# Retention, softplus and relu-squared kernel: the head works on 128 tokens as one chunk, and step 0's products come in two halves of the tokens

## The chip, the cores and the metric

The kernel runs on one core of a Trainium2 chip. The metric is device time in microseconds (us) of one execution. Engines are named TensorE (PE in the profile; PEld is its loading of weights), VectorE (DVE), ScalarE (ACT) and SyncE (SP, which here only issues DMAs). A tile in SBUF or PSUM has 128 partitions; "lower" and "upper" are partitions 0 to 63 and 64 to 127.

## The reference

Three stages, all in float32. q, k and v are (4, 8, 576, 64): batch, heads, tokens, head size. x has 2304 rows of 512 columns.

```python
# 1: retention with decay, no softmax
scores = q @ k.transpose(0, 1, 3, 2) / sqrt(64)
gamma = 1 - 2.0 ** (-5 - arange(8))                 # one per head
rel = pos[:, None] - pos[None, :]
ret = (scores * where(rel >= 0, gamma ** rel, 0)) @ v
x = ret.transpose(0, 2, 1, 3).reshape(2304, 512)
# 2: softplus layer, weights 512 x 2048 and 2048 x 512
h = x @ w1_in
x = (maximum(h, 0) + log1p(exp(-abs(h)))) @ w1_out
# 3: relu-squared layer, weights of the same shapes
r = maximum(x @ w2_in, 0)
out = (r * r) @ w2_out
```

## The kernel before, in words

Retention is computed by chunks: within a chunk by masked scores, across chunks by a running state (k times v, 64 x 64 per head). The decay is a weight on v per token and head (table `vw`) and a factor on the result (table in `cst`, one block of 256 columns for each of the nine 64-token blocks of a sequence). The layers work on tiles of 512 or 384 tokens (`TILES`). The second layer's products with float32 accuracy are three products each of rounded parts: high by high, high by low, low by high.

The weights come through SP's queue into a ring of three staging buffers (`load_w`, `pump_load`). `words` makes two passes of ScalarE and one of VectorE over a block, `split_w` then makes its high part on ScalarE and its low part on VectorE; `pump_step` does one of these stages, `pump_begin` begins blocks, `pump_end` ends them and issues the next loads.

The order on every engine is the program's (`manual_schedule`). The head (lines 982 to 1103) makes x for the first 512 tokens, in four chunks of 128. A chunk is loaded by two DMAs of 512 KB on SP's queue (line 362): q and k transposed, lower partitions the first 64 tokens, upper the second, all eight heads side by side; then k and v with tokens on partitions. The opening loads constants on ScalarE's queue, runs 18 warm products of 128 columns (`keep_warm`), spreads two rows of constants over the partitions by products with ones (`spread`, line 963), and makes the factor table from them on VectorE (`make_xw`, line 972: blocks 1, then 2 and 3, then 4 to 8). For each chunk TensorE then computes scores of 64 by 64 tokens (line 1016), the state of the first 64 tokens (line 416), and, interleaved, outputs of both halves (line 439; each half has its own products and, after the first, products with the carried state), the second half's state and the next chunk's scores. VectorE weights v (372), masks the scores (1023), scales the outputs into x (1048) and makes the low part of x (1062); ScalarE copies the state twice a chunk in two pieces (427), casts the high part of x (1052) and issues the store of x (1056). The first block of w1_in is split among the last chunk's work, blocks 1 and 2 behind it.

Then the steps begin: step j computes 12 products of 512 columns (`g1`, line 519), softplus (lines 532 to 545), part of the attention of the next tiles (`attend`), the split of the result (554, 555), and the second product of step j - 2 (`g2`, line 570). In step 0 `g1` needs all 512 tokens' high and low x and the split block 0.

## Time and profile before

| | us |
|---|---|
| three runs | 841.63, 843.45, 843.67 |
| median | 843.45 |
| profiled execution | 842.52 |
| its span, first to last instruction | 840.7 |

The profile is of one execution. "Busy" is the time in which an engine had an instruction in it; for TensorE the ends are modelled, and instructions overlap, so a row's duration of 0.22 us for a small product is its latency and the distance between starts is its cost. Each float32 product stands as two matmul instructions. PEclk is the granted clock of TensorE, 1.00 being full speed; before the first change of the clock that was recorded it reads 1.00. "Issue" in the chain of waits is time in which the engine waited for nothing that the profile shows.

### The profile page before, as it was taken

How to read it: one execution, taken by the hardware profiler on the slowest of the kernel's cores; microseconds unless marked ns; L12 is line 12 of the kernel's file. 1: busy time of each engine (PE TensorE's matmuls, PEld its weight loads, DVE VectorE, ACT ScalarE, POOL GpSimd, SP SyncE). 2: the span in 40 equal slices, each digit the busy share in tenths (PEclk: the TensorE clock that was granted, in tenths of full speed). 3: DMA queues.
4: the chain of work that ended last, by engine and by line, in shares of the span. 5: the costliest groups of instructions: out<-in, count | busy, mean ns of one | idle time of the engine just before them, and what ended most of it. 6: DMA issues, size and time to landing. Idle time of an engine off the chain costs nothing.

```text
span 840.7 us, 16953 instructions
## 1 busy us (share of the span) xinstructions
PE 820.1 (98%) x6189; PEld 731.0 (87%) x6189; DVE 700.3 (83%) x1331; ACT 473.7 (56%) x890; POOL 0.2 (0%) x4
## 2 busy tenths in 40 slices
PE   8889999999999999999999999999999999999998
PEld 7767799988788877888899999988999988999887
DVE  3688888878978888787999988899698997787876
ACT  2699899666666766666888621355321554111553
POOL 0000000000000000000000000000000000000000
PEclk9899999999999999999999999999999999999999
DMA  9556545546556674476686788898988889888885
GB/s 329 178 177 221 187 145 173 179 139 195 187 185 212 199 224 161 149 234 212 206 265 208 238 242 250 248 310 275 305 255 250 250 265 279 290 250 249 252 272 167
DMA packets 121207, 189.44 MB, mean 225 GB/s; under 512 B 10402, under 2 KB 66338, under 8 KB 121122
## 3 DMA queue, kind: packets, MB, share of 16 engines
q1 hardware_dynamic: 118848, 187.21, 70.1%
q10 hardware_dynamic: 2276, 1.14, 0.5%
q8 instruction: 50, 0.82, 0.4%
q14 instruction: 33, 0.27, 0.1%
HBM read 147.41 MB, written 40.89 MB: 224 GB/s over the span
## 4 chain that ended last, share of the span: by engine, by line
PE 82%; DVE 7%; ACT 6%; issue 2%; DMA 1%; ACTq 0%; DVEq 0%
PE acc L570 19%; PE ph L519 18%; PE py L699 9%; PE py L772 9%; PE px L699 6%; PE pz L772 6%; PE px L772 6%; PE pz L699 6%; PE po L439 2%; DVE l L542 1%; ACT l L534 1%; DVE xl L482 1%; DVE e L539 1%; PE st L416 1%; ACT e L533 1%
## 5 line engine op out<-in xcount | busy, mean ns | idle before, releaser
L519 PE MATMUL ph<-xh,wi 128*128 128x512 f32 (+1 forms) x640 | 146.7, 371 | 2.1 <-ACT l L534 1.1
L519 PEld LDWEIGHTS ph<-xh,wi 128*128 128x128 f32 x640 | 117.4, 189 | 18.8 <-issue 1.6
L570 PE MATMUL acc<-gh,woh 128*128 128x512 f32 (+1 forms) x320 | 120.1, 378 | 0.4 <-ACT woh L185 0.4
L570 PE MATMUL acc<-gl,woh 128*128 128x512 f32 (+1 forms) x320 | 118.6, 371 | 1.4 <-DVE gl L555 1.4
L570 PE MATMUL acc<-gh,wol 128*128 128x512 f32 (+1 forms) x320 | 118.1, 369 | 0.7 <-DVE wol L186 0.7
L539 DVE SCALAR_TENSOR_TENSOR e<-e 128x512 f32<-128x512 f32 (+1 forms) x80 | 51.0, 638 | 45.7 <-ACT l L534 44.9
L699 PE MATMUL py<-t,sring 128*128 128x384 f32 x432 | 88.6, 339 | 0.0
L519 PE MATMUL ph<-xl,wi 128*128 128x512 f32 (+1 forms) x320 | 78.9, 367 | 0.1
L532 ACT ACTIVATE e<-ph 128x512 f32<-128x512 f32 (+1 forms) x80 | 44.2, 552 | 58.6 <-PE ph L519 58.2
L699 PEld LDWEIGHTS py<-t,sring 128*128 128x128 f32 x432 | 74.8, 188 | 2.5 <-DVE uring L903 0.5
L752 ACT CAST gh<-g 128x384 fp32r<-128x384 f32 x84 | 43.2, 515 | 46.2 <-PE px L772 16.1
L570 PEld LDWEIGHTS acc<-gl,woh 128*128 128x128 f32 x320 | 60.1, 188 | 10.4 <-DVE gl L555 3.5
L570 PEld LDWEIGHTS acc<-gh,woh 128*128 128x128 f32 x320 | 60.0, 188 | 9.5 <-ACT woh L185 0.8
L570 PEld LDWEIGHTS acc<-gh,wol 128*128 128x128 f32 x320 | 60.1, 188 | 8.9 <-DVE wol L186 1.3
L519 PEld LDWEIGHTS ph<-xl,wi 128*128 128x128 f32 x320 | 58.7, 188 | 8.0 <-DVE xl L482 0.4
L752 ACT CAST gring<-g 128x384 fp32r<-128x384 f32 x84 | 43.2, 516 | 39.9 <-PE py L772 16.2
L899 ACT COPY uring<-px 128x384 f32<-128x384 f32 x24 | 11.5, 479 | 87.3 <-PE px L699 87.3
L699 PE MATMUL pz<-t,sring 128*128 128x384 f32 x288 | 58.3, 334 | 0.0
L699 PE MATMUL px<-t,sring 128*128 128x384 f32 x288 | 58.0, 335 | 0.0
L534 ACT ACTIVATE l<-e,cst 128x512 f32<-128x512 f32 (+1 forms) x80 | 54.5, 681 | 5.8 <-DMA part_d<-xo 1.9
L720 DVE TENSOR_TENSOR gring<-g,gring 128x384 fp32r<-128x384 f32 x84 | 46.2, 553 | 9.8 <-ACT gring L752 8.6
L720 DVE TENSOR_TENSOR g<-g 128x384 f32<-128x384 f32 x96 | 52.6, 554 | 1.5
(116 smaller groups left out, 1635.9 us busy)
## 6 DMA issues: line engine op xcount, KB each, us to landing
sring<-s2d SPq DMA_DIRECT2D x168, 256.0 KB, 3.2
sring<-o2d SPq DMA_DIRECT2D x168, 256.0 KB, 3.5
wi_raw<-in_moe_w_in_dram SPq DMA_DIRECT2D x32, 512.0 KB, 4.6
wo_raw<-in_moe_w_out_dram SPq DMA_DIRECT2D x32, 512.0 KB, 3.7
s2d<-ct SPq DMA_DIRECT2D x48, 256.0 KB, 2.7
o2d<-ct SPq DMA_DIRECT2D x48, 256.0 KB, 2.5
ring<-in_qk_t_dram SPq DMA_DIRECT2D x14, 512.0 KB, 5.2
ring<-in_kv_dram SPq DMA_DIRECT2D x14, 512.0 KB, 6.1
```

The source lines that it names most:

```text
L416: nc.tensor.matmul(st[to, h, :], lhsT=kk[:, hh, :], rhs=sv[:, hh, :], start=m == h == 0, stop=True, skip_group_check=True,)
L439: nc.tensor.matmul(po[(LO, HI)[hh % 2], hh // 2, :], lhsT=before[rows, hh, :] if carried else sv[:, hh, :], rhs=qp[:, hh, :] if carried el ...
L519: nc.tensor.matmul(ph[:, :n], lhsT=a, rhs=x, start=(j == 0), stop=(j == len(todo) - 1))
L532: nc.scalar.activation(out=e, in_=ph[:, :n], func=AF.Abs)
L534: nc.scalar.activation(out=l, in_=e, func=AF.Ln, bias=below_one, scale=1.0 + 2.0**-23)
L539: nc.vector.scalar_tensor_tensor(out=e, in0=e, scalar=-2.0, in1=e, op0=ALU.add, op1=ALU.mult)
L570: nc.tensor.matmul(acc[j][:, :n], lhsT=a, rhs=x, start=(begin and m == 0), stop=(end and m == 2))
L699: nc.tensor.matmul(ps, lhsT=a, rhs=x, start=(first and m == 0), stop=(m == len(todo) - 1), skip_group_check=True,)
L720: nc.vector.tensor_tensor(out=out, in0=a, in1=b, op=ALU.subtract)
L752: nc.scalar.copy(h, src)
L772: nc.tensor.matmul(blocks[m][:, :cols], lhsT=a[:, c], rhs=x, start=(first and p == n == 0), stop=(p == NP - 1 and n == len(todo) - 1), ski ...
L899: nc.scalar.copy(s1, px)
```

## The change

The head keeps its four chunks, but a chunk is one block of 128 tokens. q and k come as two loads of 256 KB each, heads 0 to 3 to the lower and 4 to 7 to the upper partitions, on the queues of SP and ScalarE (chunk 3 on SP alone). Scores are 128 x 128 tokens per head, masked by one 128 x 128 mask (`causal`); the state is made once a chunk from all 128 tokens and copied once (`kept_s`). Scores of even chunks go to two banks of their own, those of odd chunks to the two banks of `ps_h`. Chunk c + 1's scores stand ahead of chunk c's state. The warm products are 6 and 1 of 512 columns in place of 18, 3, 4 and 8 of 128. Blocks 4 to 8 of the factor table are made by ScalarE, four pieces of 128 x 64 each. x is stored from SP's queue. Step 0's `g1` is `early_g1`: tokens 0 to 255 within the head, 256 to 511 at its old place. `g1` of other steps is as before.

```diff
-    first = tc.tile_pool(name="first", bufs=n_first)
+    first = tc.tile_pool(name="first", bufs=2)
...
+    def early_qk(c, g, eng):
+        eng.dma_start(
+            out=qks[c][(LO, HI)[g]].rearrange("p i s h c -> p i s (h c)"),
+            in_=qk_t[2 * c:2 * c + 2].rearrange("s p i h c -> p i s (h c)")[
+                ..., g * HH * CN:(g + 1) * HH * CN
+            ],
+        )
...
+    def early_scores(c):
...
+        for hh in range(HH):
+            for s, to in enumerate((LO, HI)):
+                for g, rows in enumerate((LO, HI)):
+                    nc.tensor.matmul(
+                        pb[g][to, hh * P:(hh + 1) * P],
+                        lhsT=qks[c][rows, 1, s, hh, :], rhs=qks[c][rows, 0, :, hh, :],
...
+    def early_mask(c):
+        mixed[c] = first_pool.tile([P, H, P], F32, tag="mixed", name="mixed")
+        for g, pb in enumerate(pbs[c]):
+            n = H // len(pbs[c])
...
+            nc.vector.tensor_tensor(
+                out=mixed[c][:, g * n:(g + 1) * n], in0=pb,
+                in1=causal.unsqueeze(1).to_broadcast([P, n, P]), op=ALU.mult,
+            )
+
+    def early_states(c):
...
+        for h in range(HH):
+            for to, hh in ((LO, h), (HI, h + HH)):
+                nc.tensor.matmul(
+                    st[to, h, :], lhsT=kvs[c][:, 0, hh, :], rhs=kvs[c][:, 1, hh, :],
...
+        if c + 1 < last:
+            kept_s[c] = first_pool.tile([P, HH, D], F32, tag="kept", name="kept")
+            nc.scalar.copy(kept_s[c], st)
...
+    def early_carried(c):
+        pos[c] = ps_head.tile([P, 2, 512], F32, tag="po", name="po", bufs=1)
+        for h in range(HH if c else 0):
+            for g, rows in enumerate((LO, HI)):
+                nc.tensor.matmul(
+                    early_po(c, g * HH + h),
+                    lhsT=kept_s[c - 1][rows, h, :], rhs=qks[c][rows, 0, :, h, :],
...
+    def early_o(c):
+        for hh in range(H):
+            nc.tensor.matmul(
+                early_po(c, hh), lhsT=kvs[c][:, 1, hh, :], rhs=mixed[c][:, hh, :],
...
+    def early_keep(c):
+        nc.sync.dma_start(out=x0d[:, :, c * P:(c + 1) * P], in_=kept_of[c])
...
+    def early_g1(half):
+        if half == 0:
+            hps[0] = h_bank("ph")
+        c = slice(half * 256, half * 256 + 256)
...
+        todo = sum(todo if half else [todo[0], todo[2], todo[1]], [])
...
+    def scalar_xw(m, n):
+        for m in range(m, m + n):
+            for a in range(KD):
+                nc.scalar.activation(
+                    out=later[:, m - 1, a], in_=cst[:, C_XW + a * CN:C_XW + (a + 1) * CN],
+                    func=AF.Copy, scale=times[:, m - 1, a:a + 1],
+                )
...
+        early_qk(0, 0, nc.sync)
+        early_qk(0, 1, nc.scalar)
+        early_kv(0)
         for half in (LO, HI):
             nc.scalar.dma_start(out=cst[half, :C_XW], in_=consts[CN:P, :C_XW])
...
+        keep_warm(6)
+        early_scores(0)
+        row.append(rows_in.rearrange("p (m a b) -> p m a b", a=KD, b=CN))
+        spread_rows()
+        keep_warm(1)
+        scalar_xw(4, 2)
+        early_mask(0)
+        early_v(0)
         make_xw(1, 1)
+        early_scores(1)
+        early_states(0)
+        early_mask(1)
+        early_v(1)
+        early_carried(0)
+        early_o(0)
+        early_x(0)
+        early_scores(2)
+        early_states(1)
+        scalar_xw(6, 1)
+        early_carried(1)
+        early_o(1)
         make_xw(2, 2)
+        early_mask(2)
+        early_v(2)
+        early_x(1)
+        scalar_xw(7, 2)
+        early_scores(3)
+        early_states(2)
+        early_carried(2)
+        early_o(2)
         early_low(0)
+        early_mask(3)
+        early_v(3)
+        begin_words()
         early_keep(0)
+        early_x(2)
+        next(begun[0])
         early_low(1)
         early_keep(1)
         early_states(3)
+        early_carried(3)
+        early_o(3)
+        next(begun[0])
+        begun.clear()
+        begin_words()
+        early_g1(0)
+        early_x(3)
+        next_state(3, 1)
+        begin_words()
         early_low(2)
+        early_low(3)
         early_keep(2)
+        for made in begun:
+            next(made)
         early_keep(3)
...
-        g1(j, f, n)
+        if j == 0:
+            early_g1(1)
+        else:
+            g1(j, f, n)
```

## Rows read from the trace of the kernel before

**Rows 1.** windows: stretches; per engine busy us and instructions, then clock, DMA

```profile
10.80:31.50 20.70, 17.81 (x521) 16.72 (x520) 12.68 (x19) 9.84 (x24) 0.00 (x0) 0.92 0.62 214
...
50.00:90.00 40.00, 37.84 (x398) 30.37 (x396) 35.90 (x65) 37.27 (x67) 0.00 (x0) 1.00 0.70 235
90.00:840.00 750.00, 740.57 (x5039) 664.50 (x5039) 634.96 (x1217) 410.76 (x775) 0.00 (x0) 1.00 0.71 225
```

**Rows 2.** timeline, opening: start, duration, engine, line, operation, tiles, count

```profile
0.73 0.39 SPq L362 DMA_DIRECT2D ch<-in_qk_t_dram  x1
...
1.04 6.77 PE L946 MATMUL cold<-warm 128*128 128x128 f32 x36 [1.04 <-DVE warm L940]
...
8.60 0.64 PE L963 MATMUL rows<-rows_in,ones 1*64 1x256 f32 x2 [0.15 <-DMA rows_in<-in_consts_dram]
...
10.81 1.15 PE L1016 MATMUL pb<-ch 64*64 64x64 f32 x32
11.88 1.16 PE L946 MATMUL cold<-warm 128*128 128x128 f32 x8
12.97 0.68 PE L416 MATMUL st<-ch 64*64 64x64 f32 x16
```

**Rows 3.** chain of waits in order of time: start, duration, what

```profile
17.07 1.16 issue
...
21.57 1.45 issue
```

**Rows 4.** windows, around the stretch at the lower clock

```profile
19.50:23.30 3.80, 2.35 (x77) 2.09 (x73) 2.68 (x5) 1.98 (x5) 0.00 (x0) 1.00 0.54 183
23.30:26.80 3.50, 3.50 (x106) 3.50 (x99) 0.69 (x1) 1.03 (x3) 0.00 (x0) 0.51 0.02 5
```

**Rows 5.** timeline, last chunk and step 0's products

```profile
29.12 0.69 DVE L1048 TENSOR_TENSOR x<-po,cst 128x512 f32<-128x512 f32 x1 [0.65 <-PE po L439]
...
30.32 0.62 ACT L1052 CAST xh<-x 128x512 fp32r<-128x512 f32 x1
...
31.51 1.20 PE L519 MATMUL ph<-xh,wi 128*128 128x512 f32 x4
...
33.45 1.07 PE L519 MATMUL ph<-xh,wi 128*128 128x512 f32 x4
```

**Rows 6.** timeline, SP's issue of wo0 and ScalarE up to step 1

```profile
30.43 0.33 SPq L137 DMA_DIRECT2D wo_raw<-in_moe_w_out_dram  x1
...
31.36 0.68 ACT L152 ACTIVATE wi_raw<-wi_raw 128x512 f32<-128x512 f32 x1
...
35.27 0.60 ACT L532 ACTIVATE e<-ph 128x512 f32<-128x512 f32 x1
...
41.80 0.62 ACT L185 CAST woh<-ct 128x512 fp32r<-128x512 f32 x1 [3.31 <-DVE ct L157]
```

**Rows 7.** DMA queues and issues of the first 30 us

```profile
q8 instruction: 4, 0.07, 0.9%
...
ch<-in_qk_t_dram SPq DMA_DIRECT2D x4, 512.0 KB, 5.8
...
x0d<-x ACTq DMA_DIRECT2D x3, 256.0 KB, 2.9
```

**Rows 8.** timeline of TensorE where four quarters run

```profile
18.46 0.23 PE L439 MATMUL po<-ch,ring 64*64 64x64 f32 x2
...
18.52 0.23 PE L439 MATMUL po<-ch,ring 64*64 64x64 f32 x2
```

**Rows 9.** groups by form, VectorE: count, busy us, mean ns of one

```profile
L1023 DVE TENSOR_TENSOR ch<-pb,cst 128x512 f32<-128x512 f32 x4 | 2.8, 691 | 3.6 <-PE pb L1016 3.6
...
L972 DVE SCALAR_TENSOR_TENSOR cst<-cst,times 128x1280 f32<-128x1280 f32 x1 | 1.5, 1484 | 0.0
```

**Rows 10.** groups by form, ScalarE up to 35.3 us

```profile
L427 ACT COPY ring<-st 64x256 f32<-64x256 f32 x16 | 5.9, 366 | 11.4 <-PE st L416 11.2
...
L967 ACT COPY times<-rows 128x32 f32<-128x32 f32 x1 | 0.2, 187 | 0.4 <-PE rows L963 0.4
```

More of the change, by code (lines that the diff above doesn't have):

```diff
@@ L512, in g1 @@
                 part.append((a[:, c], x))
-        if key:
-            todo = [[w for two in zip(*todo[:2]) for w in two], todo[2]]
-        else:
-            todo = [todo[0], todo[2], todo[1]]
-        todo = sum(todo, [])
+        todo = [w for two in zip(*todo[:2]) for w in two] + todo[2]
         for j, (a, x) in enumerate(todo):
@@ L956 @@
     times = times.rearrange("p (m a) -> p m a", a=KD)
-    def spread(dst, row, shape, eng):
-        rows = ps_head.tile([P, 512], F32, tag="pb1", name="rows")[:, :shape[0] * shape[1]]
-        rows = rows.rearrange("p (a b) -> p a b", a=shape[0])
-        for half in (LO, HI):
-            one = slice(half.start, half.start + 1)
-            nc.tensor.matmul(
-                rows[half], lhsT=ones[one], rhs=row[one],
-                start=True, stop=True, skip_group_check=True,
-            )
-        eng(dst, rows)
     def make_xw(m, n):
@@ new lines, in early_o, with early_x @@
+    def early_o(c):
+        for hh in range(H):
+            nc.tensor.matmul(
+                early_po(c, hh), lhsT=kvs[c][:, 1, hh, :], rhs=mixed[c][:, hh, :],
+                start=c == 0 and hh % HH < 2, stop=True, skip_group_check=True,
+            )
+    def early_x(c):
+        m = 2 * c
+        if c < last - 1:
+            x = ew.tile([P, 512], F32, tag="e", name="x", bufs=3)
+        else:
+            x = ew.tile([P, 512], F32, tag="l", name="x")
+        kept = x.rearrange("p (a n) -> p a n", a=KD)
+        xs_of[c] = kept
+        table = cst[:, C_XW + m * 256:C_XW + (m + 2) * 256]
+        nc.vector.tensor_tensor(
+            out=x.rearrange("p (g a s b) -> p g a s b", g=2, a=2, s=2),
+            in0=pos.pop(c)[:, :, :256].rearrange("p g (a s b) -> p g a s b", a=2, s=2),
+            in1=table.rearrange("p (s g a b) -> p g a s b", s=2, g=2, a=2), op=ALU.mult,
+        )
+        nc.scalar.copy(early_at(x_hi(), c), kept)
+        kept_of.append(kept)
@@ new lines, in begin_words, with spread_rows @@
+    def begin_words():
+        count, make, args = items[n_split[0]]
+        pump_load(n_used[0] + count)
+        begun.append(make(*args))
+        next(begun[-1])
+        n_split[0] += 1
+        n_used[0] += count
+    row = []
+    def spread_rows():
+        rows = ps_head.tile([P, 2, 512], F32, tag="po", name="rows", bufs=1)
+        to = [
+            rows[:, 0, at:at + n * b].rearrange("p (a b) -> p a b", a=n)
+            for at, n, b in ((0, KD, CN), (256, SCN - 1, KD))
+        ]
+        for half in (LO, HI):
+            one = slice(half.start, half.start + 1)
+            for r, of in zip(to, (row[0][:, 0], row[0][:, 1:, :, 0])):
+                nc.tensor.matmul(
+                    r[half], lhsT=ones[one], rhs=of[one],
+                    start=r is to[0], stop=True, skip_group_check=True,
+                )
+        nc.scalar.copy(cst[:, x_first].rearrange("p (a b) -> p a b", a=KD), to[0])
+        nc.scalar.mul(times, to[1], float(D) ** 0.5)
@@ L984 @@
         for half in (LO, HI):
             nc.scalar.dma_start(out=cst[half, :C_XW], in_=consts[CN:P, :C_XW])
-        for row in (0, CN):
-            nc.scalar.dma_start(
-                out=rows_in[row:row + 1], in_=consts[row:row + 1, C_XW:]
-            )
+        for r in (0, CN):
+            nc.scalar.dma_start(out=rows_in[r:r + 1], in_=consts[r:r + 1, C_XW:])
+        early_qk(1, 0, nc.sync)
+        early_qk(1, 1, nc.scalar)
+        early_kv(1)
+        early_qk(2, 0, nc.sync)
+        early_kv(2)
@@ L999 @@
             )
-        keep_warm(18)
-        row = rows_in.rearrange("p (m a b) -> p m a b", a=KD, b=CN)
-        spread(
-            cst[:, x_first].rearrange("p (a b) -> p a b", a=KD), row[:, 0], (KD, CN), nc.scalar.copy
-        )
-        spread(times, row[:, 1:, :, 0], (SCN - 1, KD), nc.scalar.copy)
-        make_xw(1, 1)
-        keep_warm(3)
-        pbs, pos, xs_of, kept_of = {}, {}, {}, []
-        def early_scores(c, half):
-            if c not in pbs:
-                pbs[c] = in_heads(ps_head.tile([P, 512], F32, tag=f"pb{c % 2}", name="pb"))
-            return [
-                lambda h=h: nc.tensor.matmul(
-                    pbs[c][half, h, :], lhsT=chunk[c][half, 1, h, :], rhs=chunk[c][half, 0, h, :],
-                    start=True, stop=True, skip_group_check=True,
-                ) for h in range(H)
-            ]
@@ L1103 @@
         early_keep(3)
     tc.no_sync_barrier()
-    for c in range(last):
-        chunk.pop(c)
     head.__exit__(None, None, None)
```

152 lines of the change are left out of this document (75 added, 77 removed).

## The prediction

> **What bounds the kernel now.** The page has TensorE busy almost throughout, so I split the span into stretches [rows 1]. From 90 us on TensorE works 740.57 of 750 us; nothing that the change touches lies there, so that part stays as it is. From 50 to 90 TensorE, ScalarE and VectorE are all at 90 to 95%. Only the head (10.8 to 31.5 us, TensorE 17.81 of 20.70, VectorE 12.68, ScalarE 9.84) has room, and as the later work follows it at a fixed distance, a microsecond by which the head ends earlier is a microsecond of the whole, unless step 0 or 1 gets a new wait.
>
> In the head the work is serial; there I went through the timeline and the chain of waits. The first score products start at 10.81, because the warm products and then the row of constants (8.60) hold TensorE [rows 2]. Four chunks follow, each with scores, mask, first state, its copy, second state, its copy, outputs. Twice TensorE stands, for 1.16 and 1.45 us, with nothing that the profile names [rows 3], and for 3.5 us its granted clock is 0.51, the lower of its two levels (1.2 and 2.4 GHz), after a stretch in which it was busy for only 2.35 of 3.80 us [rows 4]. The last chunk's x is made at 29.12, its cast starts at 30.32, and step 0's products run from 31.51 to 34.52 [rows 5]. But ScalarE is what step 0's softplus waits for: it works from 31.36 until it takes up that softplus at 35.27 [rows 6], when the products are already done. So the forecast is the new time of that softplus.
>
> **The change part by part.** All times are for the profiled execution (span 840.7, whole 842.52 us); the median of the three runs shown is 0.9 us above it.
>
> *Opening.* 18 warm products of 128 columns become 6 of 512. Each is two instructions: 36 took 6.77 us [rows 2], 0.19 each; later 8 take 1.09 with a change of form at the end, so about 0.12 without. In pieces of 128 columns the new count is 48, 12 more: 1.4 to 2.3 us, and 0.2 for clearing a wider operand first. I take 1.4, as the last pieces are the fast ones: TensorE is free at 7.8 + 1.6 = 9.4. Scores no longer stand behind the constants, and chunk 0's q and k were to hand by about 6.5 (issue 0.73 [rows 2] plus 5.8 [rows 7]). Scores start at 9.4, not 10.81.
>
> *TensorE in a chunk.* Scores: 16 products of 128 columns, 32 instructions, going round the four quarters of the array. Where all four are in use now, a round of four instructions of 64 columns takes 0.06 us (18.46 to 18.52 [rows 8]); with 128 columns 0.12, so 8 rounds take 1.0. State: 8 products instead of 16, over all 128 tokens; 16 instructions of 64 columns that alternate between two quarters took 0.68 with their tail [rows 2], 0.5 without. Carried: 8 products of 128 columns in four quarters, 0.5. Own: 8 products over all rows, 128 columns, in two halves, 16 x 0.06 = 0.95. Together 2.9 us. If halves did not run side by side, own and state products would take double, 1.4 more a chunk; none would be cheaper than a round. I take the side-by-side figure, which [rows 2] shows for two quarters.
>
> A change of form costs too. From the eight warm products at 11.88 to the state products at 12.97 it is 1.09 us for 8 x 0.11, so 0.2 for going from the full array to quarters; from quarters to the full array it is 0.1 (scores end about 11.77, 10.81 + 1.15 less a tail of 0.19; next start 11.88) [rows 2]. The new chunk changes form four times (quarters, full rows in halves, quarters, full rows), where a chunk kept to quarters before. At 0 to 0.2 each I take 0.17: 0.7 a chunk, 2.7 in all, of which about half falls into waits for VectorE, so 1.3 on the path.
> The Trainium skill, "TensorEngine Tiling (Array Packing)", Tiling Modes, says under its key properties that changing the mode, not just the tile, drains the engine: by it all 16 changes are paid, as in the sum below. The trace shows the drain at the full array (0.1 and 0.2 us), none between quarters and halves; without it the sum would be 1.3 us lower.
>
> *The walk.* 4 x 3.6 us, less the carried part that chunk 0 hasn't (0.7), is 13.7; the constants' products and one more warm product of 512 columns take 2.3 with their changes: 9.4 + 13.7 + 2.3 = 25.4 for the last own product. VectorE beside it: the mask is now 1024 columns wide, 1.22 us by the two widths in [rows 9] (0.69 for 512, 1.48 for 1280); with v, x and the low part at 0.6 (a start every 0.6 us) that is 3.0 a chunk against TensorE's 3.6, so they are hidden, and without that cover each would cost its excess. ScalarE makes 20 pieces of 128 x 64 of the table that VectorE made in one instruction of 1.48 us: 0.19 for 32 columns and 0.37 for 256 [rows 10] put one at 0.2, 4.0 us in all, bounds 2.4 (overlapped) to 5.0. In exchange 16 state copies of 0.37 become 3 single ones and two. The pieces stand in gaps of ScalarE; only the last eight (1.6 us) delay the third state copy, to about 22.6, level with the product that overwrites what it reads.
>
> *Tail.* x of chunk 3 falls behind the low part of wi0 on VectorE and starts at 26.0. Then x 0.69, cast 0.62, low 0.69, with 0.1 between and two others ahead of the last: 28.2. The first half of step 0's products (tokens 0 to 255) needs none of this and runs before; the second half is 12 x 256 columns, 1.4 (8 x 512 took 1.94 in [rows 5]), and 0.2 tail: 29.8, against 34.52. ScalarE from the cast's end (27.3): state copies 0.75, two passes over wi2 1.3, then the casts of wi1 and wi2, the second behind VectorE's 0.69: 30.8. That is the softplus, 4.5 us before 35.27.
>
> *DMAs.* q and k come as eight loads of 256 KB to 64 partitions in runs of 1 KB, not four of 512 KB. Bounds: no slower, or half the rate. At half, 2 MB take up to 5 us more, and the last chunk lands near 18, wi0 near 20; first uses are 19 (scores 3), 21.8 (v 3) and 22.5 (wi0). I take no cost; the cover is one to two microseconds, and a loss beyond it is paid in full. The four stores of x move from ScalarE's queue to SP's, ahead of wo0, wi3 and wo1. wo0 was issued at 30.43 [rows 6], as soon as its buffer was free; now it stands behind the store of chunk 3 (27.4), and the stores (2.9 us each to landing [rows 7]) precede its data: landing near 32.5, when ScalarE is through with the softplus (32.7). A microsecond more would be lost there, but the next cast waits 3.31 us for VectorE anyway [rows 6], so up to that it costs nothing.
>
> *Unnamed waits.* Those of [rows 3] lie one chunk's 128 matmuls apart, and in 30 us four loads of instructions arrive [rows 7]. The new head has some 340 matmuls in place of 570, so I count half a wait: 0.6 us back.
>
> Sum: 4.5 - 0.6 = 3.9 us; 842.5 - 3.9 = 838.6 us (span 836.8).
>
> **The rivals.**
> 1. *More than that:* no changes of form on the path (1.3) and no unnamed wait (0.6): 836.7. For it: quarters run side by side without loss in [rows 8]. Against: TensorE is nearly full in the walk, so any wait adds.
> 2. *Halves don't run side by side:* 1.4 a chunk, 5.6 in all, 1 us of it in waits: gain 3.9 - 4.6, so 843.2, no change. For it: no row shows products of 128 rows in two halves. Against: of 64 rows they do, 16 in 0.5 [rows 2].
> 3. *The clock stays low (slower).* Only 7 of the 33 warm products remain, none after 13 us, and TensorE stops at each mask that is late. A stretch like that of [rows 4] gives away 3.5 x 0.49 = 1.7 us of products, so from the third on the gain is gone. Low from the first scores to the softplus, some 13 us of array work take twice as long; less 1.5 of waits that this covers and the gain it is 13 - 1.5 - 3.9 = 7.6 us slower: 850. For it: such a stretch came in spite of 33 warm products. Against: it followed a wait of 1.45 us and few products; the walk has no gap above 0.5 us.
> The Trainium skill, "TensorE: Matmul & The Clock Gate", HAM oscillation, has idle gaps between bursts of products bring the slow clock back; by it this rival comes if the masks leave such gaps.
> 4. *Moved, not won:* wo0 or the next chunk comes late, and steps 0 and 1 give 2 to 3 us back: 841.2. For it: SP's new order. Against: the 3.31 us of cover.
>
> **How the numbers follow.** Forecast (gain 2.6 to 5.5) 0.58, rival 1 0.14, rival 2 0.10, rival 3 0.07, rival 4 0.11. A measurement can tell 0.3%, 2.5 us, from no change. Faster by more: the forecast, rival 1 and a little of rival 4, 0.74. Within: most of 4 and 2, 0.18. Slower: rival 3 and a bad rival 2, 0.08. The range goes from rival 1 with an opening that wins its bounds and with the overlapped table pieces (another 2.4 us), 834.3, to between rivals 4 and 2, 842.3; rival 3 and the rest of rival 2 are left out.
>
> **What would show it.** The first scores at 9.4; a chunk every 3.6 us (now 4.6); own products 0.06 apart; last x at 26.0; the first softplus at 30.8 with the same 6.5 us from it to the cast now at 41.80. It is wrong if the granted clock shows 0.5 in more than one stretch before 30 us, if scores wait for a load, if TensorE stands over 1 us at the second or third chunk, or if the softplus comes 4 us earlier and the later rows don't.

## The result, and the profile after

The changed kernel takes 848.2 us (median of 9 runs, 845.65 to 851.01), the kernel before 843.45 (9 runs, 841.21 to 845.94): a ratio of 1.0066, 95% interval 1.0045 to 1.0087. It is slower, by 0.7%; the forecast was 838.6 and faster. A ratio is not the quotient of the two medians, so the two need not agree in the last digits.

The profiled execution takes 850.5 us (span 848.7), 8.0 more than that of before. Both kernels take up 80 softpluses in the same order, so the start of each first pass on ScalarE is a clock for the whole program (L532 before, L525 after). After minus before: +0.93 at step 0, then level (+0.90 at step 8), +2.45 at step 9, +4.74 at step 11, +6.36 at step 12, level until step 51, +7.60 at step 52, +8.0 from step 66 on. So one microsecond was lost ahead of step 0, where 4.5 were to be won, and seven in places that the change does not touch.

The windows of [rows 1] show the head still full of waits, with a mean granted clock of 0.84 instead of 0.92 (columns: stretch, its length, busy us and instructions of TensorE, its weight loads, VectorE, ScalarE, GpSimd, then granted clock, DMA share, GB/s):

```profile
10.80:31.50 20.70, 16.70 (x282) 13.08 (x283) 11.74 (x19) 10.53 (x33) 0.00 (x0) 0.84 0.91 264
50.00:90.00 40.00, 37.86 (x404) 30.63 (x400) 35.83 (x65) 37.22 (x67) 0.00 (x0) 1.00 0.71 230
```

The timeline of the opening answers to [rows 2] and shows why. Columns: start, duration, engine (ACTq is ScalarE's queue for DMAs), line, what is done, in brackets the wait before it and what ended it.

```profile
0.72 0.73 ACTq L976 DMA_DIRECT2D qk<-in_qk_t_dram  x1
1.48 1.28 ACTq L1150 DMA_DIRECT2D cst<-in_consts_dram  x2
2.79 0.77 ACTq L1152 DMA_DIRECT2D rows_in<-in_consts_dram  x1
4.65 0.21 ACTq L1152 DMA_DIRECT2D rows_in<-in_consts_dram  x1
7.82 0.63 ACTq L976 DMA_DIRECT2D qk<-in_qk_t_dram  x1
8.54 1.10 PE L998 MATMUL pb<-qk 64*64 64x128 f32 x32
...
12.42 0.43 PE L998 MATMUL pb<-qk 64*64 64x128 f32 x2
...
16.19 1.98 PE L998 MATMUL pb<-qk 64*64 64x128 f32 x30 [3.34 <-DMA qk<-in_qk_t_dram]
18.09 1.12 PE L1030 MATMUL st<-kv 128*64 128x64 f32 x16
19.00 1.92 PE L1054 MATMUL po<-mixed,kv 128*64 128x128 f32 x16
```

The scores of chunk 0 start at 8.54, earlier than forecast. But the upper half of chunk 1's q and k is the sixth load on ScalarE's queue, behind the constants, and the thirteenth of the two queues together. Eight loads are under way at first, four on each queue; by the semaphores in the trace, each later one waits until the load eight places ahead of it, on either queue, has landed. On ScalarE's queue the first four are issued by 3.56, the fifth at 4.65, this one at 7.82, just as the second load of constants, the fifth of all, has landed (7.80). It lands at 16.14, and TensorE stands 3.34 us in the middle of chunk 1's scores. What follows is at the lower of the two clock levels (0.5, 1.2 GHz): 30 score matmuls take 1.98 us and the 16 own products 1.92, against 1.09 for the same 16 in the next chunks. The windows show the level (columns as above):

```profile
14.00:16.00 2.00, 0.00 (x0) 0.00 (x0) 0.00 (x0) 0.00 (x0) 0.00 (x0) 0.81 1.16 205
16.00:18.00 2.00, 1.81 (x30) 1.58 (x30) 0.00 (x0) 0.00 (x0) 0.00 (x0) 0.50 1.11 231
18.00:20.00 2.00, 2.00 (x29) 1.91 (x28) 1.79 (x3) 0.37 (x1) 0.00 (x0) 0.50 1.04 348
20.00:22.00 2.00, 2.00 (x34) 1.67 (x34) 1.12 (x3) 0.31 (x1) 0.00 (x0) 0.50 1.09 347
```

The loads also move fewer bytes per microsecond. From 4 to 16 us the DMA engines are full in both kernels (the last columns: DMA share, GB/s), at 381 GB/s before and 267 in the changed kernel. The kernel before, then the changed one:

```profile
4.00:16.00 12.00, 11.36 (x187) 9.87 (x187) 4.08 (x9) 2.03 (x7) 0.00 (x0) 1.00 1.03 381
```

```profile
4.00:16.00 12.00, 8.49 (x54) 3.91 (x52) 3.08 (x8) 3.77 (x11) 0.00 (x0) 0.97 1.09 267
```

So x of the last chunk comes at 31.59 [rows 5: 29.12] and the softplus at 36.20 [rows 6: 35.27]:

```profile
31.59 0.68 DVE L1068 TENSOR_TENSOR x<-po,cst 128x512 f32<-128x512 f32 x1
32.31 0.62 ACT L1073 CAST xh<-x 128x512 fp32r<-128x512 f32 x1
...
36.20 0.60 ACT L525 ACTIVATE e<-ph 128x512 f32<-128x512 f32 x1
...
42.30 0.62 ACT L185 CAST woh<-ct 128x512 fp32r<-128x512 f32 x1 [2.70 <-DVE ct L157]
```

The later losses are of two kinds. One is the clock again. Between the softpluses of steps 7 and 8 TensorE waits for the splits that ScalarE and VectorE make of the weights and of the softplus, in both kernels in the same way: 1.32 and then 0.64 us busy in two windows of 2 us. In the kernel before the granted clock stays at 1.00 behind this dip:

```profile
88.80:90.80 2.00, 1.32 (x6) 0.69 (x4) 1.93 (x4) 2.00 (x5) 0.00 (x0) 1.00 0.54 191
90.80:92.80 2.00, 0.64 (x2) 0.34 (x3) 2.00 (x4) 2.00 (x4) 0.00 (x0) 1.00 0.00 0
92.80:94.80 2.00, 2.00 (x9) 1.63 (x10) 1.71 (x4) 1.94 (x5) 0.00 (x0) 1.00 0.27 37
```

In the changed kernel the same dip, 0.9 us later, is followed by 0.51, for 3.4 us, and step 9 comes 1.5 us later:

```profile
89.70:91.70 2.00, 1.32 (x6) 0.68 (x4) 1.93 (x4) 2.00 (x5) 0.00 (x0) 1.00 0.60 203
91.70:93.70 2.00, 0.64 (x2) 0.33 (x3) 2.00 (x5) 2.00 (x4) 0.00 (x0) 1.00 0.00 1
93.70:95.70 2.00, 2.00 (x5) 1.54 (x6) 1.72 (x4) 1.94 (x5) 0.00 (x0) 0.51 0.02 8
```

The other kind is a store that lands late. The waits of the changed kernel (engine, its instruction, what it waited for, us in total, times, longest), and then those of the kernel before:

```profile
ACT l L527 <- DMA part_d<-xo: 4.3, 1, 4.3
ACT l L527 <- DMA x2d<-xo: 3.5, 2, 3.3
```

```profile
ACT l L534 <- DMA part_d<-xo: 1.9, 1, 1.9
ACT l L534 <- DMA x2d<-xo: 1.8, 2, 1.6
```

The part sums (step 10) and x2 (step 52) leave by four stores each. ScalarE writes its logarithm into a buffer of the kind from which the second and the fourth go out (`drain_one`), and by the trace it waits until the second has landed: in the kernel before that store is issued at 103.17 and lands 2.03 us later, and the logarithm starts at 105.31. In the changed kernel the DMA view of the five microseconds from the first store has one packet of queue q8 among them, which starts 2.4 us after the first issue, and a median of 4.8 us from issue to landing (columns: queue, packets, MB, share; tiles, queue, count, KB each, us to landing):

```profile
q8 instruction: 1, 0.02, 2.3%
...
part_d<-xo SPq DMA_DIRECT2D x4, 256.0 KB, 4.8
```

In the same stretch of the kernel before no q8 row stands (its load starts 5.4 us after the first store), and the stores take 2.0 us:

```profile
part_d<-xo SPq DMA_DIRECT2D x4, 256.0 KB, 2.0
```

q8 brings instructions: 47 loads of 16 KB for 11,914 matmuls and weight loads of the changed kernel, 50 for 12,378 before, so one for about 250 of them. The change removes 464, and so the loads fall at other points of the program.

Steps 10 to 12 lose 4.0 us in all: 2.4 by this wait, 1.6 because TensorE then stands 2.67 us and the clock falls once more (0.5 for 3.4 us at 114.2). Step 52 loses 1.2 by the second wait.

### The profile page after: what moved, and what is told of

It reads as the page before. It is cut to its first block, busy times and chain, and to the rows that moved or that the text cites. A ratio compares the mean times of both kernels' runs of the same rounds, so it can differ in the third digit from the quotient of the medians.

```text
span 848.7 us, 16501 instructions
## 1 busy us (share of the span) xinstructions
PE 822.5 (97%) x5957; PEld 726.9 (86%) x5957; DVE 702.6 (83%) x1336; ACT 475.1 (56%) x899; POOL 0.2 (0%) x4
## 4 chain that ended last, share of the span: by engine, by line
PE 79%; DVE 8%; ACT 8%; DMA 3%; issue 2%; ACTq 0%; DVEq 0%
PE acc L563 17%; PE ph L512 16%; PE py L692 9%; PE py L765 9%; PE px L692 6%; PE pz L765 6%; PE px L765 6%; PE pz L692 6%; ACT l L527 1%; DVE l L535 1%; DVE e L532 1%; PE po L436 1%; ACT e L526 1%; DVE xl L479 1%; ACT e L525 1%
## 5 line engine op out<-in xcount | busy, mean ns | idle before, releaser
L532 DVE SCALAR_TENSOR_TENSOR e<-e 128x512 f32<-128x512 f32 (+1 forms) x80 | 51.0, 638 | 52.7 <-ACT l L527 51.7
L525 ACT ACTIVATE e<-ph 128x512 f32<-128x512 f32 (+1 forms) x80 | 44.2, 553 | 61.5 <-PE ph L512 60.8
L692 PEld LDWEIGHTS py<-t,sring 128*128 128x128 f32 x432 | 74.9, 188 | 2.6 <-DVE uring L896 0.5
L713 DVE TENSOR_TENSOR gl<-g,gh 128x384 fp32r<-128x384 f32 x84 | 46.6, 556 | 9.1 <-ACT gh L745 8.0
```

The costliest lines, as they stand in the source:

```text
L525: nc.scalar.activation(out=e, in_=ph[:, :n], func=AF.Abs)
L532: nc.vector.scalar_tensor_tensor(out=e, in0=e, scalar=-2.0, in1=e, op0=ALU.add, op1=ALU.mult)
L692: nc.tensor.matmul(ps, lhsT=a, rhs=x, start=(first and m == 0), stop=(m == len(todo) - 1), skip_group_check=True,)
L713: nc.vector.tensor_tensor(out=out, in0=a, in1=b, op=ALU.subtract)
```

## Experiments

Theory A: three things cost the time: the late load, the clock that falls behind waits, and instruction loads that fall into stores. Rivals: the new products or loads are slow as such; or the win is absorbed by full engines later.

Results first; "low" is the sum of the stretches with a granted clock of 0.5 in the first 120 us of the profiled execution (the openings of e13 to e15 are told of below), "softplus" the start of step 0's. Each ratio is to runs of the kernel before that were made along with the version (their medians lie between 841.8 and 843.5).

| kernel | median us | ratio to before, 95% | softplus | low, us |
|---|---|---|---|---|
| before | 843.45 | 1 | 35.27 | 6.8 |
| changed | 848.2 | 1.0066 (1.0045 to 1.0087) | 36.20 | 17.1 |
| e1 load of chunk 1 on SP | 845.09 | 1.0039 (1.0027 to 1.0051) | 32.06 | 10.2 |
| e2 short warm products | 845.07 | 1.0040 (1.0027 to 1.0052) | 35.18 | 13.7 |
| e3 = e1 + e2 | 841.54 | 0.9995 (0.9980 to 1.0011) | 32.03 | 10.2 |
| e5 = e3 + products in step 0's gap | 839.93 | 0.9977 (0.9964 to 0.9990) | 31.22 | 6.8 |
| e6 = e5 + products in step 8 | 840.19 | 0.9972 (0.9958 to 0.9985) | 32.28 | 0 |
| e7 = e3, step 0 not in halves | 841.94 | 1.0003 (0.9984 to 1.0021) | 32.84 | 10.2 |
| e8 = e3 + chunk 2's load on SP | 840.88 | 0.9989 (0.9968 to 1.0011) | 31.53 | 10.2 |
| e10 = e6 + e8 | 839.73 | 0.9964 (0.9948 to 0.9981) | 32.53 | 3.4 |
| e11 = e5 + e8 | 840.88 | 0.9972 (0.9956 to 0.9988) | 31.53 | 3.4 |
| e12 = e10, opening as changed | 841.28 | 0.9968 (0.9950 to 0.9986) | 32.06 | 3.4 |
| e13 = e10, opening in 40 | 848.27 | 1.0044 (1.0014 to 1.0074) | 41.96 | - |
| e14 = e10, opening in 43 | 850.36 | 1.0081 (1.0061 to 1.0102) | 40.96 | - |
| e15 = e10, opening in 46 | 851.60 | 1.0091 (1.0061 to 1.0121) | 44.59 | - |
| e4 before + 72 TensorE instructions | 844.17 | 1.0033 (1.0017 to 1.0048) | 36.23 | 3.4 |
| e9 before + 28 | 845.29 | 1.0022 (1.0003 to 1.0041) | 35.88 | 13.7 |
| e16 before + 40 | 846.22 | 1.0035 (1.0013 to 1.0056) | 35.92 | 13.7 |
| e17 before + 44 | 847.41 | 1.0059 (1.0039 to 1.0078) | 36.04 | 13.7 |

### The late load and the count of instructions: e1, e2, e3

```diff
-        early_qk(1, 1, nc.scalar)      # e1 and e3
+        early_qk(1, 1, nc.sync)
-        keep_warm(6)                   # e2 and e3: the same columns,
+        keep_warm(24, P)               # 72 TensorE instructions more
```

> The changed kernel with one load moved: the upper half of chunk 1's q and k is issued on SP's queue, behind the lower half, not on ScalarE's. Theory L (that load's late issue holds TensorE 3.8 us and brings the slow clock): scores of chunk 1 start by 12.5 us, no clock of 0.5 between 14 and 22 us, first softplus from 36.2 to 31 to 32, time 4 to 5 us under the changed kernel's 848.2, so 843 to 844, as the later store waits stay. Theory C (too few warm products let the clock fall): the clock still falls before 22 us and the softplus stays above 34.5; time over 846. Theory D (loads to 64 partitions are slow as such): another load is late in its place, chunk 2's or 3's, softplus 33 to 36.

> The changed kernel with its opening cut finer: 24 warm products of 128 columns for 6 of 512, the same columns, 72 more instructions on TensorE. Theory F (a load of TensorE's instructions, one per 256 of them, falls since the change into the stores of part_d at 106.6 us and delays them; ScalarE waits 4.3 us instead of 1.9 and the clock falls behind it): the load comes some 36 products earlier, the wait at the first ln of that step is back under 2.5 us, time 2.4 to 4 us under the changed kernel, 844 to 846; the first softplus stays at 36 to 36.5. Rival (the stores are slow for another reason, x's stores on SP's queue or chance): the wait stays over 4 us, time 848 within 1.5.

> The two edits together, chunk 1's load on SP's queue and 24 warm products of 128. Theories L and F: the gains add up, 4 to 5 and 2.4 to 4 us: 839 to 842, which is 2 to 4 us faster than the kernel before. If either is wrong, its part is missing: 843 to 846.

e1 takes the first softplus from 36.20 to 32.06; no clock of 0.5 is left between 10 and 33 us, and chunk 1's scores run without the wait:

```profile
12.97 1.10 PE L998 MATMUL pb<-qk 64*64 64x128 f32 x32
...
32.06 0.60 ACT L525 ACTIVATE e<-ph 128x512 f32<-128x512 f32 x1
```

That is 4.1 us for one load in another queue, the eighth of all now and not the thirteenth; the transfers as such are no faster (263 GB/s from 4 to 16 us). Of the 4.1, 1.2 are lost again at step 1 and the wait for the part sums stays (3.7 us), so that the time is 1.1 us above what theory L gave. e2 leaves the late load in place and gains as much: the instruction loads now start at 95.3 and 115.4 us, and the wait for the part sums is 2.0. In e3 both stand side by side. e1 and e3 have the same first softplus within 0.03 us and the same distance to before until step 10; at step 11 they part by 1.6, and the load that starts 2.4 us after the first store in e1 starts 10.8 after it in e3. Both edits are needed, and they only make the changed kernel level with the one before: the time is within what was expected of e3, the 2 to 4 us won against the kernel before are not there.

### The clock: e5, e6

```diff
+            if c == last and s == 0:    # step 0, between its two score visits
+                keep_warm(3, 448, ps_acc.tile([P, 512], F32, tag="at", name="cold"))
+                for _ in range(2 if key == 6 and j == 0 and m < 2 else 0):   # e6
+                    nc.tensor.matmul(acc[j][:, :n], lhsT=zeros, rhs=h[:, :n],
+                                     start=False, stop=False)
```

> On top of the version with both edits (chunk 1's second load of q and k on SP's queue, 24 short warm products; 841.5 us): three products of a cleared tile (448 columns) on TensorE between the two mask visits of step 0, where it stood 2.64 us just before its granted clock read 0.5 for 6.8 us. Theory A (the low clock after this gap gives back what the head won: step 0 to step 1 took 8.29 us, not the 7.06 of the kernel before): no reading of 0.5 at 33 to 40 us, softplus of step 1 near 39.2 instead of 40.32, the whole 1.0 to 1.3 us less, 840.3. Theory B (the stretch comes from the products' own pattern, not the gap): the clock still falls, time unchanged. Theory C (the won 1.2 us are absorbed by a later wait, as ScalarE and VectorE are full from 50 to 90 us): step 1 earlier, whole time unchanged.

> The one before, and four more products with a cleared operand in step 8 of the loop (they add zero to the sums), in the waits of 0.89 and 0.70 us near 89 us after which the granted clock read 0.5 for 3.4 us at 91.4. Theory A: that stretch goes too, step 8 to 9 takes 5.05 us as in the kernel before (6.60 with the stretch), and the whole is 2.5 to 2.9 us less than 841.5, near 838.8. Theory B (the four products delay the sums and the casts behind them, or the clock falls elsewhere instead): no gain over the one before, or a loss up to 0.5 us.

In e3 TensorE is busy 0.10 of 2 us before step 1's products, which then run at 0.5 (windows, columns as above):

```profile
31.00:33.00 2.00, 0.10 (x4) 0.00 (x0) 1.91 (x4) 1.69 (x4) 0.00 (x0) 1.00 0.94 349
33.00:35.00 2.00, 1.26 (x17) 1.17 (x18) 1.38 (x4) 1.97 (x4) 0.00 (x0) 0.58 1.07 370
35.00:37.00 2.00, 2.00 (x5) 1.61 (x6) 1.92 (x4) 0.25 (x1) 0.00 (x0) 0.50 1.01 385
```

In e5 useless products fill the gap, the clock stays at 1.00 until 40.2, and the softplus of step 1 comes at 37.85, 6.63 us after step 0's, not 8.29:

```profile
30.00:32.00 2.00, 2.00 (x17) 1.19 (x12) 1.90 (x4) 1.70 (x4) 0.00 (x0) 1.00 0.85 300
32.00:34.00 2.00, 1.82 (x21) 1.01 (x20) 1.81 (x4) 1.97 (x4) 0.00 (x0) 1.00 1.06 376
34.00:36.00 2.00, 2.00 (x11) 1.61 (x10) 1.89 (x5) 0.44 (x1) 0.00 (x0) 1.00 0.98 385
```

That is theory A, and the win stays to the end: e5 is faster than before by 0.23%. In e6 the clock reads 1.00 behind the dip of step 8 too, and step 8 to 9 takes 5.01 us (6.48 in e5, 5.05 before). But the whole is no shorter than e5's: its head ends 1.1 us later (softplus at 32.28, not 31.22; TensorE waits 0.48 us for the row of constants and 1.34 for chunk 2's q and k, against none and 1.05), and at step 67 it loses 1.3 us to x2 stores, into which an instruction load falls (at 420.6 us, stores from 417.65). In e5 the load starts at 423.8 and nothing is lost.

### Halves and loads: e7, e8

```diff
-        early_g1(0)                     # e7: and g1(j, f, n) in every step
-        early_qk(2, 1, nc.scalar)       # e8
+        early_qk(2, 1, nc.sync)         # e8: right behind early_qk(2, 0, nc.sync)
```

> The version with both edits (841.5 us), but step 0's products not in two halves of the tokens: all twelve of 512 columns after the last cast, as in the kernel before. Theory A (the halves win what the prediction said, 1.4 us of products out of the tail): the first softplus moves from 32.03 to 33.4 and the whole to 842.8. Theory B (ScalarE takes up the softplus at 32.03 only because it is busy with the words of wi1 until then; the products end by 31.7 either way): first softplus within 0.3 us of 32.03, and as TensorE then stands less ahead of step 1, perhaps no low clock at 33 us: 840.3 to 841.5.

> The version with both edits (841.5 us), with chunk 2's second load of q and k on SP's queue as well, right behind its first. Theory A (that load is late because ScalarE's queue issues it at 8.0 us, behind four loads of constants): TensorE's wait of 1.17 us for q and k of chunk 2 goes, the first softplus comes at 30.9 to 31.2 instead of 32.03. Theory B (the loads as such are slow, 1 KB pieces to 64 partitions; the order only shifts the wait to chunk 3 or to the first weights): first softplus within 0.4 us of 32.03.

Without the halves the first softplus comes 0.8 us later (32.84 against 32.03), but that is the clock's and not the halves'. In e7 TensorE stands 1.99 us ahead of the undivided products, the granted clock then reads 0.5 for 3.4 us from 28.3 on, and the first eight products take 3.68 us. ScalarE is free at 31.34 and waits 1.49 us for them:

```profile
28.14 3.68 PE L512 MATMUL ph<-xh,wi 128*128 128x512 f32 x8 [1.99 <-ACT xh L1073]
...
32.84 0.60 ACT L525 ACTIVATE e<-ph 128x512 f32<-128x512 f32 x1 [1.49 <-PE ph L512]
```

In the kernel before all twelve took 3.0 us [rows 5]; at that pace e7's would have ended near 31.2 (an estimate), before ScalarE was free, as in theory B. So no gain of the halves is shown beyond the low clock that they keep out of this place. Of the whole nothing can be measured either: step 1 of e7 comes at 39.33, before e3's 40.32. e8 removes the wait for chunk 2's q and k (1.2 us in e3) and the softplus gains 0.5, between A and B. By step 6 it then loses 2.7 us to before: an instruction load starts at 63.4, 2.6 us after SP issued q and k of a later chunk (60.79), those take 8.5 us to landing (6.7 in e3), TensorE waits for that chunk, and its clock reads 0.5 for 6.8 us from 68.9 on. That the instruction load is what delays them is argued from this order, not tested. On the timeline:

```profile
69.30 0.37 PE L388 MATMUL pb<-ring 64*64 64x64 f32 x2 [2.30 <-DMA ring<-in_qk_t_dram]
```

### Where an instruction load falls: e4, e9, e12 to e17

```diff
-        keep_warm(18)                   # e4, e9, e16, e17: on the kernel before,
+        keep_warm(15)                   # products of 32 columns:
+        tiny(21)                        # 21 in e4, 10 in e9, 13 in e16, 14 in e17
-        keep_warm(24, P)                # on e10: e12 keep_warm(6),
+        keep_warm(40, 76)               # e13 this, e14 (43, 72), e15 (46, 66)
```

> The kernel before, with 15 of its 18 opening warm products and 21 tiny ones of 32 columns, so that TensorE has 72 instructions more ahead of the stores and nothing else is changed. Theory F: the instruction load that came at 107.1, behind the stores of part_d, now falls into them (it should start near 102 to 105); ScalarE's wait for that store grows from 1.9 to 3.5 to 4.5 us, time 2 to 4 us above the kernel before, 845.5 to 847.5. Rival: the wait stays at 1.9 and the time within 1 us of the kernel before.

> The kernel before (842.1 us) with its 18 warm products replaced by 15 and 10 small ones of 32 columns: 28 TensorE instructions more, nothing else. In the kernel before an instruction load starts at 107.1 us, 5.4 us after the first store of a part sum was issued (101.73); with 72 instructions more it moved to 99.5 and missed those stores. Theory A (a load that starts 2 to 3 us after the first of these stores delays them; in the changed kernel it cost ScalarE a wait of 4.3 us instead of 1.9): with 28 more it starts near 104, ScalarE's wait for the stores is 3.5 us or more, steps 10 to 12 take 1.5 to 4 us longer, the whole 1.5 to 4 us more. Theory B (the wait belongs to the new head's later transfers, not to the count of instructions): that wait stays near 1.9 us and the time within 1 us of 842.1, except for what the opening itself shifts.

> The version with all mended, but with the changed kernel's own opening: 6 products of 512 columns in place of 24 of 128, the same columns in 72 TensorE instructions fewer. There an instruction load starts at 90.6 us and the next at 109.3, and the part sums are stored from 98.51 us on; with 72 fewer the first should move by 11 us, as it did between the two versions with and without the short products, to 101, which is 2.5 us after the first store (2.4 in the changed kernel). Theory A (an instruction load amid these stores costs the wait): ScalarE's wait for the stores rises from 1.8 to 3.7 us or more, step 10 to 11 takes 7.2 us or more instead of 5.58, the whole 1.5 to 2.5 us more than 839.7, while the first softplus stays within 0.8 us of its place. Theory B (the wait came from the changed kernel's late head and low clock): the wait stays at 1.8 to 2.0 us and step 10 to 11 at 5.6, wherever the load falls.

> The version with all mended, the opening's 24 products of 128 columns cut into 40 of 76: 64 TensorE instructions more. The load that started at 109.3 us should start near 102.1, about 3.4 us after the first store of a part sum. Theory A (a load amid these stores costs the wait): ScalarE's wait for them 2.5 to 4 us, step 10 to 11 6.2 to 7.3 us instead of 5.58. Theory B (something else): wait 1.7 to 2.0, step 10 to 11 5.6.

> The same with 43 of 72 columns: 76 instructions more, the load near 101, 2.4 us after the first store, as in the changed kernel. Theory A: ScalarE's wait 3.5 to 4.3 us, step 10 to 11 7.2 us or more, the whole 1.5 us or more above 839.7. Theory B: wait 1.7 to 2.0, step 10 to 11 5.6.

> The same with 46 of 66 columns: 88 instructions more, the load near 99.8, 1.2 us after the first store. Theory A: ScalarE's wait 2 to 4 us, as part of the stores lies behind the load. Theory B: wait 1.7 to 2.0.

> The kernel before with 15 warm products and 13 small ones: 40 TensorE instructions more. Theory A: the load starts 2 to 3 us after the first store of a part sum, ScalarE's wait for the stores is 3.5 us or more (1.8 to 1.9 in the kernel before and in the two versions beside it), step 10 to 11 takes 7.2 us instead of 5.64. Theory B: that wait and that step stay.

> The same with 14 small ones, 44 more: the load 1.5 to 2.5 us after the first store; the two theories as for the one before.

All eight missed what they aimed at: the load near the part sums started 2.7 us before the first store (e4), 0.1 before it (e12) or 4.2 to 6.7 after it, and in all of them the wait stayed at 1.8 to 2.0 us. In e9 and e16, with the load at 4.3 and 4.2, the third store did land late (4.5 and 4.4 us after its issue, 2.3 in the kernel before), but ScalarE waits for the second, which had landed. The count of instructions does not place a load finely enough by hand. But the same loads pass the x2 stores of step 52 too, and there they hit. By the distance of the load from the first store of that drain, in all 19 traces:

| load after the first x2 store, us | ScalarE's wait, us | traces |
|---|---|---|
| 3.1 to 3.3 | 3.0 to 3.4 | changed, e1, e4, e12, e16, e17 |
| 2.6 to 2.8 | 2.3 to 2.8 | e2, e3, e5, e7, e8, e11 |
| 1.0, 1.1, 5.7, or before it | 1.5 to 1.8 | before, e6, e9, e10, e13, e14, e15 |

For the part sums it is 2.4 us, 4.3 and 3.7 us of wait (changed, e1), and everywhere else 1.7 to 2.0. In e16 the head is the old one, with 40 TensorE instructions more. Its DMA view from the first x2 store on, and then that of the kernel before:

```profile
x2d<-xo SPq DMA_DIRECT2D x4, 256.0 KB, 4.1
```

```profile
x2d<-xo SPq DMA_DIRECT2D x4, 256.0 KB, 2.2
```

So at these two places a load some 2.4 to 3.3 us behind the first store costs 0.7 to 2.4 us, whatever the head is like. Theory A holds for this wait by these traces; taking the load away from the part sums took the wait away (e2, e3), but no run brought it back on purpose. At the x2 stores near 175 to 187 us that rule does not hold: a load 2.5 us ahead of the first store goes with a wait of 0.9 to 1.2 us (e13 to e15), one 2.7 us ahead with 0.2 (before).

e16 and e17 answer a further question. They compute what the kernel before computes, by the old head, and lose 3.5 and 4.7 us at the medians against the kernel before beside them: a low clock of 6.8 us instead of 3.4 from 37 us on (1.2 us at step 1), one of 3.4 us at 74.9 or 95.7 (1.5 us at step 9 in e17), and the wait at step 52 (1.2 to 1.3). e9 loses 1.3 us at step 4, behind a low clock at 59.0. These are losses of the changed kernel's kind, without its head. They come with the count of TensorE's instructions or with the 0.6 to 0.8 us by which the other warm products move the head's end; these runs do not separate the two.

e13 to e15 missed in another way: the opening kept the slow pace of its start to its end, and the first softplus came 9.4, 8.4 and 12.1 us later than in e10. Their profiled executions took 848.88, 847.01 and 849.92 us against 839.49: 9.4, 7.5 and 10.4 more. A delay of the head does go through to the end nearly whole, as the prediction had it. The opening of e10 and that of e13 on the timeline, the same columns cut into 48 and 80 matmuls:

```profile
1.45 7.13 PE L944 MATMUL cold<-warm 128*128 128x128 f32 x48 [1.45 <-DVE warm L938]
```

```profile
1.45 17.35 PE L944 MATMUL cold<-warm 128*128 128x76 f32 x80 [1.45 <-DVE warm L938]
```

### A version that beats both: e10, e11

> The changed kernel with all that helped: q and k of chunks 1 and 2 on SP's queue, 24 short warm products, three products in the gap of step 0, four products that add zero in step 8. Theory A (late loads, low clock and instruction loads are all that the change lost): first softplus near 31.2, no low clock to 100 us, softplus of step 12 near 108.7 (112.83 before), the whole 837.5 to 839.5, where the prediction for the change was 838.6. Theory B (each shift brings a new dip or a new collision of an instruction load with stores further on): no better than the versions with three products in the gap, 840.

> The one before without the four products in step 8. Theory A: the clock falls once near 88 us (1.5 us), the whole is 1.0 to 1.5 us above the one before. Theory B: no difference, or the other way round, as the shift by 16 matmul and weight-load instructions lets an instruction load fall elsewhere (the four products' version lost 1.3 us at 420 us, where a load started amid x2d stores).

e10 takes 839.73 us, 0.36% less than before; it is within B's 840 as much as at the upper end of A. Of what A named, the first softplus (32.53) and the clock (0.5 for 3.4 us at 42.2) missed, and the softplus of step 12 comes at 109.6. Ahead of the first softplus TensorE has a wait of 1.50 us for the row of constants and one of 1.43 that the profile does not name, and e10 loses 1.3 us at step 67 to the same load at 420.6 as e6. In e11 the low clock comes at 70.3, not near 88, and the time does not differ from e10's by more than the two intervals allow.

## Why the prediction was wrong

*Opening: right, and better than forecast.* Scores start at 8.54 (forecast 9.4).

*TensorE in a chunk: right.* In the rows of e3 scores take 1.10, state 0.69, carried 0.67, own 1.09 (forecast without tails 1.0, 0.5, 0.5, 0.95). Three of the four changes of form in a chunk cost the 0.17 that I took; in e3, where nothing else is late, the weight loads show it between quarters and halves too. The fourth, from state to carried products, shows 0.07 (18.79 to 18.86), too little for the profile to call it a wait:

```profile
18.24 0.55 PEld L1030 LDWEIGHTS st<-kv 128*64 128x64 f32 x16 [0.17 <-issue]
...
19.45 0.85 PEld L1054 LDWEIGHTS po<-mixed,kv 128*64 128x64 f32 x16 [0.17 <-issue]
...
20.48 0.86 PEld L998 LDWEIGHTS pb<-qk 64*64 64x64 f32 x32 [0.17 <-issue]
```

The Trainium skill, "TensorEngine Tiling (Array Packing)", Tiling Modes, says that a change of mode drains the engine; the trace agrees at three of the four, and [rows 2] could not show it for these two modes. From 17.21 to 20.48 a chunk of e3 takes 3.27 us (forecast 3.6). Rival 2 is out: two halves run side by side, or own products would have taken 1.9.

*The walk: a small term off.* Eight table pieces take 2.02 us in e3, 0.25 each, so twenty take 5.1, at my upper bound of 5.0, not 4.0. They hold the third state copy until 23.76 (forecast 22.6) and TensorE for 0.35 us.

*Tail: right.* From the last x to the softplus 4.6 us, in the changed kernel (31.59 to 36.20) and in e3 (27.40 to 32.03); forecast 4.8. From the softplus to the cast behind it 6.10 (42.30), forecast 6.5: the stores on SP's queue cost nothing here. But ScalarE alone sets this length; the halves of step 0's products are not shown to win any of it (e7).

*DMAs: here it failed in the head.* "I take no cost; the cover is one to two microseconds, and a loss beyond it is paid in full." I priced the loads by their bytes and looked at the last ones: chunk 3, wi0. The late one was the second of four chunks, and by its place: sixth on ScalarE's queue, thirteenth of all. TensorE had worked up to it by 12.9, and it landed at 16.14. It cost 4.1 us (e1), by the wait of 3.34 and the clock behind it. That only eight loads are under way could be read before the change: SP issued four up to 2.11 us, and the fifth, the ninth of the two queues, at 4.89, when the first constants on ScalarE's queue had landed (4.87), though SP's own first load was there at 4.65. The rate is the term that I put at nothing: 267 GB/s from 4 to 16 us against 381, about 30% less, between my two bounds. Whether the 64 partitions or the 1 KB runs make it, no run separates. From issue to landing q and k took 6.4 us on SP and 9.0 on ScalarE's queue for 256 KB, where [rows 7] has 5.8 for 512 KB; part of that is standing behind other loads. At the lower rate the order still decides which load is late: the wait of 1.2 us that is left in e3 is again for a load on ScalarE's queue, and goes with its place (e8).

*"That part stays as it is": here it failed behind the head.* I ended the forecast at the first softplus, and let the later work follow at a fixed distance. Of the 8 us, 7.1 came behind it: 1.5 at step 9 by the clock, 4.0 at steps 10 to 12 by a late store and the clock, 1.2 at step 52 by a late store, 0.4 in small pieces. Each is a place with little room that held in the kernel before by where things happened to stand; that none was lost there was luck and not cover. The distance held only where neither late stores nor the clock struck: e13 to e15.

*Unnamed waits.* I counted instruction loads as something that TensorE waits for (0.6 us won). In the changed kernel, e1 and e3 no unnamed wait above 0.3 us is left in the first 130 us, where the kernel before has 1.16 and 1.45, so 2.6 us went, not 0.6; e8 and e10 have 1.1 and 1.4 us of them again, so this is not a sure gain of the new head. Instead the loads cost as traffic: 464 instructions fewer moved them against the stores.

*The rivals.* Rival 3 gave 850 and the low clock as its cause, with a chance of 0.07. The measured 848.2 is near it, but by luck. Right in kind: 17.1 us of low clock in the first 120, where before had 6.8. But it did not come from the masks, which leave no gap worth naming; it came behind a late load, and at dips that both kernels have, and part of the time was lost to stores. Two of the signs that I had named as showing me wrong came: scores that wait for a load, and TensorE standing over 1 us at the second chunk. The Trainium skill, "TensorE: Matmul & The Clock Gate", HAM oscillation, has idle gaps between bursts bring the slow clock back. The trace agrees at 14 to 16 us and in step 0 (e5); but the same dip at 91 us left the clock at 1.00 in one kernel and at 0.51 in the other, so the gap alone does not tell.

With the load in time, short products in the opening and the gap of step 0 filled (e5), the kernel is 0.23% faster than before, half of what I forecast; with chunk 2's load and step 8 mended too (e10) 0.36%.

## What to carry to other kernels

Price a load by its place, not by its bytes alone: count what is issued ahead of it on all queues and which of those has to land before it can start, for every chunk and not only the last. Here eight were under way, and the thirteenth waited for the fifth. In a kernel whose time is full of waits just covered, a change in the count of TensorE's instructions can shift instruction loads and clock dips far behind it; 40 more (13 small useless products in place of 3) cost 0.35%. So compare step by step along the whole program, separate what the change does from what the shift does by shifting the unchanged kernel, and claim no gain below half a per cent from the one stage alone.

## What the hardware did that was not expected

- Of the two queues together eight loads are under way, and each later issue waits on a semaphore for the landing of the load eight places ahead, on whichever queue that was. ScalarE's fourth issue ends at 3.56 and the fifth starts at 4.65, SP's at 3.69 and 5.90. It looks like a limit of four for each queue; but in the kernel before SP's fifth load waits for one of ScalarE's queue, and the waits stand in the issuing instructions.
- One instruction load of 16 KB amid four stores of 256 KB goes with a median landing of 4.8 us, not 2.0, though it takes only 1.9 itself. Why it is so much more stays open.
- The granted clock reads 1.00 from the first row on, but it does not tell TensorE's pace at the start. Of 128 columns 9 matmuls fall into the stretch from 1.5 to 3.5 us of e10 and 20 into that from 5.5 to 7.5: the pace doubles within the opening. With 76 columns (e13) it stays at 10 to 12, and the scores behind it still take 1.99 us, not 1.10. So a level ahead of the first change doesn't show in that column; the pace of equal instructions does.

The windows of e10 and then of e13 for the last point (columns: stretch, length, TensorE's busy us and instructions, granted clock, DMA share, GB/s):

```profile
1.50:3.50 2.00, 2.00 (x9) 1.00 0.57 136
5.50:7.50 2.00, 2.00 (x20) 1.00 1.00 309
```

```profile
1.50:3.50 2.00, 2.00 (x10) 1.00 0.59 159
5.50:7.50 2.00, 2.00 (x12) 1.00 1.07 312
```
